# Softmax chain split between GpSimd and VectorE, units begun earlier, batch 1 loaded in 2 KB packets with v one block further ahead

## The chip, the cores and the metric

The kernel runs on one core of a Trainium2 chip. The metric is the time of one execution on the device, in microseconds (us). A core has several engines that run side by side (in the profile before, three of them are each busy for 85 to 95% of the same span): TensorE (PE in the profile; PEld is its weight load), VectorE (DVE), ScalarE (ACT), GpSimd (POOL) and SyncE (SP, which here only issues DMAs).

## The reference

Two layers follow one another, for 4 batches of 6208 rows with 256 channels:

```python
qn = q / (norm(q, axis=1) + 1e-6);  kn = k / (norm(k, axis=1) + 1e-6)   # norms over the 6208 rows
s  = kn.transpose(0, 2, 1) @ qn / tau                                    # 256 x 256 per batch
a  = exp(s - s.max(-1)); a /= a.sum(-1) + 1e-9
x  = v @ a                                                               # 6208 x 256 per batch
# channel mix, on x:
xk = mu_k * x + (1 - mu_k) * x_prev;  xr = mu_r * x + (1 - mu_r) * x_prev
out = sigmoid(xr @ w_r) * (relu(xk @ w_k) ** 2 @ w_v)                    # w_k: 256 x 1024
```

The matrix `a` of a batch is needed before the first row of that batch can be made, and it needs all rows of q and k of that batch.

## The kernel before

The rows of v are taken in 48 blocks of 512 rows, 12 to a batch (the 64 rows left over in each batch are put through in a last, shorter block). While the blocks of batch b go through the channel mix, the covariance of batch b+1 is built beside them in small *units*. One unit is 128 rows of q and k: two PE matmuls of 256 columns, and for every second unit a squaring on ACT and an addition on VectorE (for the norms). A block is written as eight steps (j = 0 to 7), and `slots` says at which steps a unit is put in. When the last unit of a batch is done, a *chain* of pieces is queued, one per step: it turns the sums into `a`. In short: `evac` copies the covariance out of PSUM, where this kernel's matmuls write it (`s_ps` in the profile); `fold` and `norms` sum the squares, `roots` copies these sums; `invert` makes the inverse norms and two diagonal matrices of them, `rq_d`; `turn` multiplies by these; `exp`, `shares` and `weigh` make the softmax.

```python
def invert():                                        # before, batches 1 to 3: all on GpSimd
    eng = nc.gpsimd if b else nc.vector
    if b:
        eng.tensor_tensor(rn, rn, half, op=OP.pow)   # rn is 128x4: root
    eng.tensor_scalar_add(rn, rn, 1e-6)
    if b:
        eng.tensor_tensor(rn, rn, minus, op=OP.pow)  # inverse
    else:
        eng.reciprocal(rn, rn)
    for h in range(2):                               # two 128x128 diagonals
        eng.tensor_scalar_mul(rq_d[:, h * P:(h + 1) * P], ident_f, rn[:, h:h + 1])
...
# the chain; `turn` is the PE product s_sb * rq_d that needs the diagonals, `weigh` writes a
return [evac, fold, None, None, norms, roots, invert, None, None, None, turn, exp, shares, weigh]
...
# q and k of a group of four units lie in SBUF as [unit, q|k, channel]: a DMA writes 512 B at a time.
# Groups for which apart() is true lie as [q|k, unit, channel]: 2 KB at a time,
# but here a squaring of two units is then two ACT instructions.
def apart(b, g):
    return b == 1 and g in (1, 2, 3)
...
if apart(b, g):
    for i in range(2):
        nc.scalar.activation(t[:rows, :, i * C:(i + 1) * C], rows_at(qk, b, g, i)[:rows, s:s + 2], AF.Square)
else:
    nc.scalar.activation(t[:rows], qk[:rows, s:s + min(n, 2)].rearrange("p s i c -> p s (i c)"), AF.Square)
...
# v: loaded by GpSimd, then transposed by a DMA that SP issues; x_half of block n runs in steps 0 and 2 of block n-2
if j == 0 and 4 <= i + 5 < NBLK - 1: v_load(i + 5)
if j == 5 and 4 <= i + 4 < NBLK - 1: v_transpose(i + 4)
...
# an addition of squares (VectorE) is issued at most at j = 1, 6, 7 (and at j = 2 when a chain waits for it)
```

## Time and profile before

| | before |
|---|---|
| time, median of 3 runs | 517.62 us (516.86 to 518.31) |
| span of the profile | 518.0 us |
| PE busy in the span | 494.2 us (95%) |
| GpSimd busy | 117.8 us |
| a block without units / with four / with six | 8.68 / 9.56 / 10.05 us |
| block 9, where batch 1's `turn` stands | 13.80 us |

The first part of the page (busy time of each engine, its share of the span, number of instructions) of the kernel before:

```profile
PE 494.2 (95%) x3478; PEld 337.3 (65%) x3540; DVE 438.4 (85%) x713; ACT 447.5 (86%) x906; POOL 117.8 (23%) x158
```

PE has little room: nearly everything that can be won is a hole in its row. The next view is the table of windows; here and below I cut the windows so that each is one block, from the first weight load of xr of that block to that of the next. The columns are named in the first line; (x73) counts instructions, PEclk is the granted clock of TensorE as a share of full speed. The three windows are block 5 (six units), block 7 (six units) and block 9 (five units and the `turn`) of the kernel before:

```profile
core 0: us, PE busy (x) PEld busy (x) DVE busy (x) ACT busy (x) POOL busy (x), PEclk, DMA share, GB/s
107.01:117.06 10.05, 10.00 (x73) 6.95 (x73) 10.05 (x16) 9.64 (x20) 2.40 (x4) 1.00 1.46 171
...
127.24:137.23 9.99, 9.88 (x71) 7.03 (x72) 9.99 (x16) 9.96 (x21) 1.49 (x2) 1.00 1.33 188
...
147.18:160.98 13.80, 11.14 (x78) 7.80 (x78) 8.72 (x14) 9.62 (x24) 10.19 (x12) 1.00 0.93 142
```

In blocks 5 and 7 of the kernel before PE is busy all but 0.05 to 0.1 us, and about that much is a matmul whose record the trace lost (725 records of one matmul line with 784 weight loads), not idleness. VectorE is busy for the whole block too: two engines are at their limit at once. In block 9, PE is idle for 2.66 us. The reason stands in PE's timeline there (start, length, then engine, line, operation, shapes, count, and in brackets the idle time before it and what ended it):

```profile
147.94 0.38 PE L182 MATMUL s_ps<-qk 128*128 128x256 bf16 x2
150.65 0.49 PE L275 MATMUL st_ps<-rq_d,s_sb 128*128 128x128 f32 x2 [2.33 <-POOL rq_d L263]
151.42 0.94 PE L275 MATMUL st_ps<-rq_d,s_sb 128*128 128x128 f32 x6 [0.28 <-POOL rq_d L263]
```

PE waits 2.33 and 0.28 us for the diagonals `rq_d`. GpSimd's timeline of the same stretch shows why they are late:

```profile
143.02 1.51 POOL L256 TENSOR_TENSOR rn<-rn,half 128x4 f32<-128x4 f32 x1 [10.97 <-ACT rn L251]
144.63 1.82 POOL L257 TENSOR_SCALAR rn<-rn 128x4 f32<-128x4 f32 x1
146.53 2.32 POOL L259 TENSOR_TENSOR rn<-rn,minus 128x4 f32<-128x4 f32 x1
148.96 2.41 POOL L263 TENSOR_SCALAR rq_d<-ident_f,rn 128x128 f32<-128x128 f32 x2
```

From the start of the first to the end of the last, these small steps take 8.3 us. In batch 0 VectorE does the same add, reciprocal and diagonals in 0.17, 0.18 and 2 x 0.28 us. For batches 2 and 3 GpSimd needed 5.6 and 4.9 us, and PE lost only about 0.3 and 0.15 us.

### The profile page before, as it was taken

Reading aid. Unit: us, or ns where it says so; the run is one execution under the profiler, and the core shown is the slowest. Engines: PE = TensorE matmul, PEld = TensorE weight load, DVE = VectorE, ACT = ScalarE, POOL = GpSimd, SP = SyncE. Lnnn points to the kernel's source line nnn. Section 1 sums busy time; section 2 is a strip of 40 time slices with the busy share of each in tenths; the row PEclk is TensorE's granted clock in tenths of the full one; section 3 lists DMA queues with packets and bytes.
Section 4 is the critical chain, followed back from the end, with each engine's and each line's share of the span. In section 5 each row is a group of like instructions: output and inputs, shape, how many; then the busy total and the mean of one; then the engine's idle time right before and its main releaser. Section 6 shows DMA issues by size and latency. Waiting matters only on the chain. (4 is left out here: it accounts for less than half of the span.)

```text
span 518.0 us, 9424 instructions
## 1 busy us (share of the span) xinstructions
PE 494.2 (95%) x3478; PEld 337.3 (65%) x3540; DVE 438.4 (85%) x713; ACT 447.5 (86%) x906; POOL 117.8 (23%) x158
## 2 busy tenths in 40 slices
PE   3979999999979999999999999999999999999996
PEld 2455666676656676667666666667666666666665
DVE  3555899999968999999988999999978888887884
ACT  5886999999969999999989999999878787878884
POOL 0034342322175221321155131210042101000000
PEclk9979999999999999999999999999999999999999
DMA  8989999999959999999559999965339686524123
GB/s 320 410 285 191 180 167 185 204 192 174 169 106 168 221 172 180 157 164 165 105 92 197 218 183 166 188 116 131 62 96 190 100 149 102 127 63 121 42 82 101
DMA packets 140373, 83.45 MB, mean 161 GB/s; under 512 B 50660, under 2 KB 135976, under 8 KB 140328
## 3 DMA queue, kind: packets, MB, share of 16 engines
q0 software_dynamic: 63504, 33.01, 51.5%
q1 hardware_dynamic: 76656, 49.72, 40.8%
q8 instruction: 27, 0.44, 0.4%
q14 instruction: 18, 0.15, 0.1%
q10 hardware_dynamic: 168, 0.13, 0.1%
HBM read 78.71 MB, written 25.43 MB: 201 GB/s over the span
## 5 line engine op out<-in xcount | busy, mean ns | idle before, releaser
L431 ACT ACTIVATE kr<-kT_ps 128x512 bf16<-128x512 f32 (+1 forms) x392 | 234.7, 607 | 36.9 <-PE kT_ps L426 28.6
L463 PE MATMUL vr_ps<-w_v_sb,kk 128*128 128x256 bf16 x1536 | 231.2, 273 | 0.5
L426 PE MATMUL kT_ps<-xk,w_k_sb 128*128 128x512 bf16 (+1 forms) x725 | 218.8, 377 | 0.7 <-DVE xk L411 0.5
L463 PEld LDWEIGHTS <-kk 128*128 128x128 bf16 x1536 | 149.1, 98 | 59.7 <-DVE kk L444 2.0
L473 DVE SCALAR_TENSOR_TENSOR res<-res,vr_ps 128x256 f32<-128x256 f32 x192 | 80.2, 418 | 48.1 <-ACT res L472 47.8
L444 DVE TENSOR_TENSOR kk<-kr 128x1536 bf16<-128x1536 bf16 (+2 forms) x148 | 117.4, 793 | 1.7 <-ACT kr L431 1.7
L426 PEld LDWEIGHTS <-w_k_sb 128*128 128x128 bf16 x784 | 75.8, 98 | 29.4 <-issue 1.2
L169 DVE TENSOR_TENSOR acc<-acc,sq 128x1024 f32<-128x1024 f32 x69 | 84.3, 1221 | 0.0
L182 PE MATMUL s_ps<-qk 128*128 128x256 bf16 x392 | 74.8, 293 | 5.4 <-DVE qk L142 5.4
L472 ACT ACTIVATE res<-vr_ps 128x256 f32<-128x256 f32 x192 | 76.9, 400 | 1.3 <-PE vr_ps L463 1.3
L459 PE MATMUL vr_ps<-w_r_sb,xr 128*128 128x256 bf16 x384 | 73.3, 272 | 3.3 <-DVE res L473 0.6
L411 DVE SCALAR_TENSOR_TENSOR xr<-delta,mu_t,xT 128x512 bf16<-128x512 bf16 x96 | 71.7, 749 | 0.0
L411 DVE SCALAR_TENSOR_TENSOR xk<-delta,mu_t,xT 128x512 bf16<-128x512 bf16 x96 | 71.6, 747 | 0.0
L165 ACT ACTIVATE sq<-qk 128x1024 f32<-128x1024 bf16 (+1 forms) x67 | 70.8, 1057 | 0.0
L459 PEld LDWEIGHTS <-xr 128*128 128x128 bf16 x384 | 37.6, 98 | 45.6 <-issue 2.0
L357 ACT CAST xT<-xT_ps 128x512 bf16<-128x512 f32 x94 | 55.6, 591 | 10.5 <-PE xT_ps L355 10.5
L136 POOL DMA_DIRECT2D qk<-in_q_dram x39 | 28.1, 721 | 157.0 <-ACT kr L431 127.1
L355 PE MATMUL xT_ps<-vT,a_sb 128*128 128x512 bf16 x188 | 55.9, 379 | 0.8 <-DVE vT L338 0.8
L182 PEld LDWEIGHTS <-qk 128*128 128x128 bf16 x392 | 39.9, 104 | 17.7 <-issue 6.3
L318 POOL DMA_DIRECT2D v_bf<-in_v_dram x48 | 37.5, 782 | 59.5 <-DMA vT<-v_bf 56.4
L401 DVE TENSOR_TENSOR delta<-xT 128x1024 bf16<-128x1024 bf16 x48 | 33.0, 688 | 1.9 <-ACT xT L357 1.8
L144 ACT ACTIVATE qk<-f 128x1024 bf16<-128x1024 f32 (+2 forms) x28 | 26.1, 948 | 8.7 <-DMA f<-in_q_dram 5.2
(85 smaller groups left out, 208.4 us busy)
## 6 DMA issues: line engine op xcount, KB each, us to landing
out_dram<-res SPq DMA_DIRECT2D x47, 512.0 KB, 5.0
v_bf<-in_v_dram POOLq DMA_DIRECT2D x48, 256.0 KB, 7.0
qk<-in_q_dram POOLq DMA_DIRECT2D x36, 256.0 KB, 7.5
qk<-in_k_dram POOLq DMA_DIRECT2D x36, 256.0 KB, 8.1
f<-in_q_dram SPq DMA_DIRECT2D x11, 512.0 KB, 8.6
f<-in_k_dram SPq DMA_DIRECT2D x11, 512.0 KB, 9.7
vT<-v_bf SPq DMA_TRANSPOSE x44, 6.5
f<-in_q_dram SPq DMA_DIRECT2D x2, 256.0 KB, 9.1
```

What stands on the lines that cost most here:

```text
L165: nc.scalar.activation(t[:rows], qk[:rows, s:s + min(n, 2)].rearrange("p s i c -> p s (i c)"), AF.Square)
L169: nc.vector.tensor_tensor(sums[b], sums[b], t, op=OP.add)
L182: nc.tensor.matmul(s_ps[:, ih, :], rows_at(qk, b, g, 0)[:rows, s, ih * P:(ih + 1) * P], rows_at(qk, b, g, 1)[:rows, s, :], start=t0 and ih ...
L355: nc.tensor.matmul(xT_ps, a_sb[:, b, ih, dh * P:(dh + 1) * P], vT[:, :, ih, :], start=ih == 0, stop=ih == 1)
L411: nc.vector.scalar_tensor_tensor(o[:, dh], st[i, "d"][:, dh], mu[:, dh:dh + 1], st[i, "x"][:, dh, :M], op0=OP.mult, op1=OP.add)
L426: nc.tensor.matmul(kT_ps[:, :m], w_k_sb[:, dh, fh * P:(fh + 1) * P], xk[:, dh, :m], start=dh == 0, stop=dh == 1)
L431: nc.scalar.activation(kr, kT_ps[:, :m], AF.Relu, scale=0.5 ** 0.5)
L444: nc.vector.tensor_tensor(st[i, "kk"][:, fh // 4 * 4 + lo:fh + 1, :m], kr, kr, op=OP.mult)
L459: nc.tensor.matmul(vr_ps[:, D:], xr[:, dh, s * P:(s + 1) * P], w_r_sb[:, dh, :], start=dh == 0, stop=dh == 1)
L463: nc.tensor.matmul(vr_ps[:, :D], kk[:, fh, s * P:(s + 1) * P], w_v_sb[:, fh, :], start=fh == 0, stop=fh == 7)
L472: nc.scalar.activation(res[:, s], vr_ps[:, D:], AF.Tanh, scale=0.5)
L473: nc.vector.scalar_tensor_tensor(res[:, s], res[:, s], 1.0, vr_ps[:, :D], op0=OP.add, op1=OP.mult)
```

## The change

Its intent is to take GpSimd's slow small steps out of the chain (only the power of the roots stays there, and `shares`, which the change does not touch), to begin the chain earlier so that nothing waits for it, to load batch 1 in fewer, larger packets, and to load and transpose v one block earlier. The diff, cut to its core:

```diff
-        return b == 1 and g in (1, 2, 3)
+        return b == 1 and g > 0
...
+        def pow2():
+            nc.gpsimd.tensor_tensor(rn, rn, half, op=OP.pow)
+
         def invert():
-            eng = nc.gpsimd if b else nc.vector
-            ... (as shown above)
+            nc.vector.tensor_scalar_add(rn, rn, 1e-6)
+            nc.vector.reciprocal(rn, rn)
             for h in range(2):
+                nc.vector.tensor_scalar_mul(rq_d[:, h * P:(h + 1) * P], ident_f, rn[:, h:h + 1])
...
-        return [evac, fold, None, None, norms, roots, invert, None, None, None, turn, exp, shares, weigh]
+        return [evac, fold, None, None, norms, roots, pow2, None, invert, None, None, turn, exp, shares, None, weigh]
...
-        v_bf = p2.tile(..., tag="v_bf", bufs=5)          # and vT: bufs=4
+        v_bf = p2.tile(..., tag="v_bf", bufs=6)          # and vT: bufs=5
...
-    FOLD = 13
+    FOLD = 15
...
-            if j == 0 and 4 <= i + 5 < NBLK - 1:
-                v_load(i + 5)
+            if j == 0 and 4 <= i + 6 < NBLK - 1:
+                v_load(i + 6)                            # and v_transpose(i + 5) for v_transpose(i + 4)
...
-            if (i, j) in ((-1, 6), (0, 4)):
+            if (i, j) in ((-1, 5), (0, 4)):              # PE transposes of v blocks 2 and 3
...
-            elif i < 8:
-                slots = (1, 2, 3, 4, 5, 7)
+            elif i < 7:
+                slots = (1, 2, 3, 4, 5, 7) if i < 3 else (1, 2, 3, 4, 5, 6, 7)
+            elif i == 7:
+                slots = (1, 2, 7)
+            elif (i - 7) % NB == 0:
+                slots = (5, 7)
             else:
-                slots = (3, 5, 7) if (i - 8) % NB == 0 else (1, 3, 4, 5, 7) if (i - 8) % NB < 3 else (1, 3, 5, 7)
+                slots = (1, 3, 4, 5, 7) if (i - 7) % NB in (1, 3, 6, 9) else (1, 3, 5, 7)
```

More of the change, by code (lines that the diff above doesn't have):

```diff
@@ L251, in roots @@
                 nc.scalar.copy(rn, bank[b][:, C:C + 4])
+        def pow2():
+            nc.gpsimd.tensor_tensor(rn, rn, half, op=OP.pow)
         def invert():
-            eng = nc.gpsimd if b else nc.vector
-            if b:
-                eng.tensor_tensor(rn, rn, half, op=OP.pow)
-            eng.tensor_scalar_add(rn, rn, 1e-6)
-            if b:
-                eng.tensor_tensor(rn, rn, minus, op=OP.pow)
-            else:
-                eng.reciprocal(rn, rn)
+            nc.vector.tensor_scalar_add(rn, rn, 1e-6)
+            nc.vector.reciprocal(rn, rn)
             for h in range(2):
-                eng.tensor_scalar_mul(rq_d[:, h * P:(h + 1) * P], ident_f, rn[:, h:h + 1])
+                nc.vector.tensor_scalar_mul(rq_d[:, h * P:(h + 1) * P], ident_f, rn[:, h:h + 1])
             if inv_tau != 1.0:
-                eng.tensor_scalar_mul(rk, rk, inv_tau)
+                nc.vector.tensor_scalar_mul(rk, rk, inv_tau)
         def evac():
@@ L316, in v_load @@
         b, t = blocks[i]
-        v_bf = p2.tile([P, S, C], BF16, name="v_bf", tag="v_bf", bufs=5)
+        v_bf = p2.tile([P, S, C], BF16, name="v_bf", tag="v_bf", bufs=6)
         nc.gpsimd.dma_start(v_bf, v[b, t * M:(t + 1) * M, :].rearrange("(s p) c -> p s c", p=P))
@@ L323, in v_transpose @@
         v_bf = st.pop((i, "v"))
-        vT = p2.tile([P, S, 2, P], BF16, name="vT", tag="vT", bufs=4)
+        vT = p2.tile([P, S, 2, P], BF16, name="vT", tag="vT", bufs=5)
         nc.sync.dma_start_transpose(vT.rearrange("c s h p -> c (s h) p"), v_bf.rearrange("p s c -> p (s c)"))
@@ L336, in go @@
         def go():
-            vT = p2.tile([P, S, 2, P], BF16, name="vT", tag="vT", bufs=4)
+            vT = p2.tile([P, S, 2, P], BF16, name="vT", tag="vT", bufs=5)
             evac(vT, vT_ps)
@@ L649 @@
                 mix(i + 1, "xr", int(j > 0))
-            if (i, j) in ((-1, 6), (0, 4)):
+            if (i, j) in ((-1, 5), (0, 4)):
                 v_transpose_pe(i + 3, nc.vector.tensor_copy)()
-            if j == 5 and 4 <= i + 4 < NBLK - 1:
-                v_transpose(i + 4)
+            if j == 5 and 4 <= i + 5 < NBLK - 1:
+                v_transpose(i + 5)
             if i == -1 and j in (5, 6):
```

## The prediction

> **What bounds the kernel now.** TensorE's streaming. The page has PE busy 95% of 518.0 us; the windows view 19.8 to 19.9 of every 20 us from 60 to 140 us and from 180 us on, clock 1.00. In the timeline matmuls start 0.11 us (256 columns) or 0.21 us (512) apart. By the output stores a block takes 8.68 us without covariance units (a unit = two 256-column matmuls), 9.55 with four, 10.05 with six. Only holes can be won:
> - Chain of batch 1 (timeline): PE waits from 148.0 to 150.65 us for rq_d from GpSimd, and 0.28 more: about 2.8 us. GpSimd: power 1.51, add 1.82, power 2.32, diagonals 2.41. Batches 2 and 3 lose only 0.3 and 0.15 us there.
> - At 55 us PE waits 0.83 us for VectorE's copy vT.
> - Batch 1's blocks: VectorE is never idle from 80 to 140 us. Its start-to-start times per block (4 res 0.33, 3 adds 1.136, 4 mixes 0.662, delta 0.60, squares 0.87 + 2 x 0.60) sum to 10.05 us, exactly the block; PE alone needs about 9.98 and waits some 0.05 for kk.
>
> [...] GpSimd's four-element add took 0.69 or 1.83 us.
>
> **What the change does.**
> - Inverse and diagonals on VectorE: 0.17 + 0.18 + 2 x 0.28 us (as in batch 0) in place of some 6.5 us on GpSimd; one power (1.2 to 1.5 us) stays. Norms to rq_d: about 6 us instead of 10.5; the turn comes seven steps (8.5 us) after the norms. So it waits for nothing: -2.8, -0.3, -0.15 us.
> - Units earlier: 7 per block in blocks 3 to 6, then 3 and 5; PE's work is the same in sum. But at most three adds are issued per block, so the fold waits to step 7 of block 7, and blocks 7 and 8 carry three adds each (before: three and one), plus fold (0.6) and inverse (0.7). VectorE then needs 10.65 and 10.75 us where PE needs 9.3 and 9.8; 0.6 us was regained in blocks 3 to 6. PE should lose 1 to 2 us there: most of what the stall gives back.
> - 2 KB packets: nine more groups are squared as two 512-column ACT instructions (0.52 us each, start to start) instead of one of 0.947: +0.09 x 18 = 1.7 us of ACT, which then needs about 10.1 us of a 10.2 us block; loss 0 to 0.5 us. PE waits for no q/k load before, so the packets give nothing themselves.
> - v one block further ahead: PE waits for no transposed load now: insurance, 0.
> - Transposes of v block 2 a step sooner: v landed at 49.7 us, needed at 51.4: -0.5 us.
>
> **Sum.** -2.8 - 0.5 (start) - 0.45 (batches 2, 3) - 0.6 (small vr_ps and kk waits) + 1.5 (VectorE, blocks 7, 8) + 0.2 (ACT): -2.7 us. Predicted **514.9 us**, 80% range **512.8 to 517.0**. Faster by over 2%: 0.01; within 2%: 0.97; slower: 0.02.
>
> **What would show it.** PE's waits for rq_d gone; GpSimd busy below 105 us; blocks 3 to 6 at 10.2 us; blocks 7 and 8 longer than 9.33 and 9.77 us with VectorE never idle; PE's wait at 55 us below 0.4 us.
>
> **What would make it wrong.** VectorE's lag reaching rq_d; ACT falling behind in blocks 3 to 6 (up to +2 us); VectorE's backlog absorbed by buffers (513 us); earlier v loads delaying q/k loads at the start.

The sum: -2.65 us, rounded to -2.7, from 517.6 to 514.9.

## More of the kernel before

One more line, which I passed over when I predicted and which turned out to matter, from the view of the tile vT (the transposed v): the time of its DMA transposes from issue to landing.

```profile
DMA to landing us min/median/max: 3.9/6.5/13.0
```

## The result, and the profile after

The time after was 514.26 us in the median (514.06 to 515.71, 4 runs), before 517.54 us (516.86 to 518.31, 4 runs). A ratio here is always the mean time of one kernel's runs over that of the other's runs of the same rounds, so it is not quite the ratio of the medians that I quote. The ratio is 0.9942, with a 95% interval of 0.9919 to 0.9965. The predicted 514.9 us lies 0.6 us off.

The span of the profile fell by more, 5.5 us, and a part of that is chance: the run of the kernel before that was profiled took 520.04 us, more than any of its four timed runs. I split every span at the first weight load of the up projection (w_k). What comes before is the phase in which DMA loads the first batch; it took 45.6 to 48.1 us in the profiles, with no order among kernels that share this code. What comes after, called the *main part* below, repeats: the changed kernel, profiled twice, gave 466.29 and 466.28 us, and one of the experiments, also twice, 465.77 and 465.75. Before, it was 470.17 us. So the change is worth 3.9 us in the main part of these traces; the kernel before has one trace only, and its wait for GpSimd varies by 2 us from trace to trace (see e11 below), so the 3.0 us by the ratio of the runs are the better figure.

The same part of the page for the changed kernel:

```profile
PE 494.6 (97%) x3540; PEld 336.7 (66%) x3540; DVE 439.7 (86%) x725; ACT 450.1 (88%) x924; POOL 99.9 (19%) x146
```

GpSimd is busy for 17.9 us less. PE at the turn of batch 1, and the chain's steps on the other two engines (from their timelines):

```profile
146.80 0.59 PE L352 MATMUL xT_ps<-vT,a_sb 128*128 128x512 bf16 x2
147.23 1.05 PE L272 MATMUL st_ps<-rq_d,s_sb 128*128 128x128 f32 x8
...
141.27 1.08 POOL L254 TENSOR_TENSOR rn<-rn,half 128x4 f32<-128x4 f32 x1 [15.55 <-ACT rn L251]
...
144.82 0.16 DVE L257 TENSOR_SCALAR rn<-rn 128x4 f32<-128x4 f32 x1
145.02 0.18 DVE L258 RECIPROCAL rn<-rn 128x4 f32<-128x4 f32 x1
145.23 0.48 DVE L260 TENSOR_SCALAR rq_d<-ident_f,rn 128x128 f32<-128x128 f32 x2
```

There is no wait in front of the turn: the diagonals are done at 145.7 us, and PE gets there at 147.2. But the windows of blocks 5, 7 and 8 show a new hole:

```profile
105.61:115.86 10.25, 10.25 (x76) 7.16 (x75) 10.25 (x16) 10.25 (x24) 2.81 (x4) 1.00 1.30 190
...
126.19:137.16 10.97, 9.80 (x67) 6.37 (x66) 10.97 (x17) 9.94 (x21) 0.00 (x0) 1.00 1.33 203
137.16:148.34 11.18, 11.18 (x88) 7.99 (x86) 11.11 (x21) 9.87 (x23) 3.36 (x4) 1.00 1.19 198
```

Block 5, now with seven units, has PE, VectorE and ACT all busy for its whole 10.25 us. Block 7 takes 10.97 us, of which PE is busy 9.80; without a wait it would need 9.43 (I take 8.67 us for a block without units and 0.218 for a unit, from the undisturbed blocks; this window holds 3.5 units). PE waits there for the results `res` of the block, which VectorE makes from ACT's output:

```profile
130.89 0.59 PE L423 MATMUL kT_ps<-xk,w_k_sb 128*128 128x512 bf16 x2
132.31 0.38 PE L456 MATMUL vr_ps<-w_r_sb,xr 128*128 128x256 bf16 x2 [0.82 <-DVE res L470]
```

And the landing of the transposes:

```profile
DMA to landing us min/median/max: 3.1/9.3/22.4
```

The slowest has gone from 13.0 to 22.4 us. The four issued from 57 to 90 us, in batch 1's blocks, took 18.5 to 22.4 us; before, those of that phase took 9.3 to 13.0 (as far as the trace has their landing).

Where the 3.9 us came from, by what each stretch lost against PE's own need (PE's own time for the norms and the turn, some 1.3 us per batch in both kernels, is in these sums):

| stretch | lost before | lost after | gain |
|---|---|---|---|
| main part up to block 0 (time, not loss) | 8.73 | 8.12 | 0.6 |
| blocks 0 to 2 | 1.1 | 1.5 | -0.4 |
| blocks 3 to 6 | 0.5 | 0.3 | 0.2 |
| block 7 (new hole) | 0.0 | 1.5 | -1.5 |
| blocks 8 to 11 (chain of batch 1) | 5.3 | 1.7 | 3.6 |
| blocks 19 to 23 (chain of batch 2) | 2.4 | 1.7 | 0.7 |
| blocks 30 to 33 (chain of batch 3) | 2.2 | 1.5 | 0.7 |

Two questions were open. Which part of the change brings the gain, and which only shifts it? And what causes the hole in block 7: VectorE's additions, as I had predicted (theory A), or ACT, which has no idle time left in blocks 3 to 6 because of the split squares (theory B)?

### The profile page after: what moved, and what is told of

The parts are those of the page before. It is cut to its first block, busy times and chain, and to the rows that moved or that the text cites. A ratio compares the mean times of both kernels' runs of the same rounds, so it can differ in the third digit from the quotient of the medians. Undisturbed runs are those within 1.5% of the kernel's fastest.

```text
span 512.5 us, 9496 instructions
## 1 busy us (share of the span) xinstructions
PE 494.6 (97%) x3540; PEld 336.7 (66%) x3540; DVE 439.7 (86%) x725; ACT 450.1 (88%) x924; POOL 99.9 (19%) x146
## 3 DMA queue, kind: packets, MB, share of 16 engines
q0 software_dynamic: 56592, 33.01, 50.0%
## 4 chain that ended last, share of the span: by engine, by line
PE 85%; DMA 6%; DVE 4%; ACT 4%; issue 1%; SPq 0%; DVEq 0%
PE vr_ps L460 31%; PE kT_ps L423 30%; PE vr_ps L456 8%; PE xT_ps L352 7%; PE s_ps L182 6%; DMA f<-in_k_dram 6%; ACT kr L428 1%; DVE acc L169 1%; DVE xk L408 1%; DVE kk L441 1%; PE st_ps L272 1%; ACT sq L163 1%; ACT xT L354 1%; DVE delta L398 1%; PE junk_ps L513 0%
## 5 line engine op out<-in xcount | busy, mean ns | idle before, releaser
L423 PE MATMUL kT_ps<-xk,w_k_sb 128*128 128x512 bf16 (+1 forms) x784 | 231.2, 377 | 0.4 <-DVE xk L408 0.2
L182 PE MATMUL s_ps<-qk 128*128 128x256 bf16 x392 | 73.5, 289 | 6.5 <-DVE qk L142 6.5
L354 ACT CAST xT<-xT_ps 128x512 bf16<-128x512 f32 x94 | 55.3, 589 | 12.1 <-PE xT_ps L352 12.1
L136 POOL DMA_DIRECT2D qk<-in_q_dram x39 | 26.3, 675 | 143.6 <-ACT kr L428 62.5
L165 ACT ACTIVATE sq<-qk 128x1024 f32<-128x1024 bf16 (+1 forms) x49 | 50.8, 1036 | 0.0
```

What stands on the lines that cost most here:

```text
L182: nc.tensor.matmul(s_ps[:, ih, :], rows_at(qk, b, g, 0)[:rows, s, ih * P:(ih + 1) * P], rows_at(qk, b, g, 1)[:rows, s, :], start=t0 and ih ...
L354: nc.scalar.copy(xT[:, dh, 1:], xT_ps)
L423: nc.tensor.matmul(kT_ps[:, :m], w_k_sb[:, dh, fh * P:(fh + 1) * P], xk[:, dh, :m], start=dh == 0, stop=dh == 1)
```

## The experiments

There were twelve kernels in three calls; those of one call shared a chip and the runs of the kernel before. On these chips the kernel before took 519.69, 517.88 and 518.77 us in the median.

| label | what it is | median us | ratio to before (95%) | main part us | block 7 us |
|---|---|---|---|---|---|
| before | | 517.5 to 519.7 | 1 | 470.17 | 9.99 |
| after | the change | 514.26 | 0.9942 (0.9919 to 0.9965) | 466.29 | 10.97 |
| e8_after_again | the change | 514.66 | 0.9945 (0.9922 to 0.9968) | 466.28 | 10.97 |
| e1_old_packets | change, packets undone | 513.55 | 0.9895 (0.9872 to 0.9919) | 465.93 | 10.62 |
| e2_inverse_only | before, VectorE inverse alone | 514.09 | 0.9897 (0.9875 to 0.9918) | 466.30 | 9.99 |
| e3_sooner_only | change, inverse on GpSimd | 519.94 | 1.0003 (0.9975 to 1.0031) | 471.16 | 10.71 |
| e4_two_adds_less | change, two additions left out | 513.69 (one run) | | 465.89 | 10.30 |
| e5_one_square | change, one ACT square per pair | 513.73 | 0.9935 (0.9907 to 0.9963) | 465.46 | 10.62 |
| e6_v_as_before | change, v no further ahead | 519.33 | 1.0035 (1.0011 to 1.006) | 471.97 | 10.72 |
| e7_parts_chosen | parts chosen | 513.30 | 0.992 (0.99 to 0.994) | 465.77 | 9.99 |
| e7_again | the same | 513.95 | 0.9915 (0.9888 to 0.9941) | 465.75 | 9.99 |
| e9_turn_step_1 | e7, turn one step sooner | 512.95 | 0.9902 (0.9874 to 0.993) | 465.21 | 9.99 |
| e10_both_less | e1 and e4 together | 513.28 (one run) | | 465.19 | 9.73 |
| e11_packets_only | before, packets alone | 522.24 (one run) | | 474.30 | 9.99 |

### The inverse alone (e2_inverse_only)

The kernel before, with the inverse and diagonals moved to VectorE, all else as it was; the turn keeps its place.

```diff
-        return [evac, fold, None, None, norms, roots, invert, None, None, None, turn, exp, shares, weigh]
+        return [evac, fold, None, None, norms, roots, pow2, None, invert, None, turn, exp, shares, weigh]
```
(with `pow2` and `invert` as in the change)

> The kernel before with one part of the change: power on GpSimd, inverse and diagonals on VectorE; same slots, same place of the turn. Theory A (the wait for GpSimd's rq_d is all that could be won from the chain, and the earlier start costs 1.5 us in block 7): PE's wait at the turn of batch 1 falls from 2.6 us to 0 to 0.5 us, blocks 1 to 7 stay at 10.05 us, the time is 2.5 to 3.5 us below before, so as good as the whole change or better by up to 1 us. Rival (the earlier start is needed): the turn still waits over 1 us for rq_d from VectorE, time 515.5 us or more.

PE's timeline at the turn of batch 1 in this kernel:

```profile
146.16 0.38 PE L182 MATMUL s_ps<-qk 128*128 128x256 bf16 x2
146.38 1.06 PE L272 MATMUL st_ps<-rq_d,s_sb 128*128 128x128 f32 x8
```

The wait is gone without any earlier start, block 7 has no hole (9.99 us), and the main part is 466.30 us, the same as the whole change. This confirms the theory: this one part brings what the whole change brings. (By the runs the ratio is even lower than the change's, but it was measured on another chip, and the intervals are wide; I do not build on that difference. The 5.6 us between the medians are also more than the 2.5 to 3.5 I had expected.) The two sums agree partly by chance: e2 has neither the 0.6 us that the change gains up to block 0 nor the hole that it pays in block 7.

### The earlier start alone (e3_sooner_only)

The changed kernel with the inverse back on GpSimd.

```diff
-  [evac, fold, None, None, norms, roots, pow2, None, invert, None, None, turn, exp, shares, None, weigh]
+  [evac, fold, None, None, norms, roots, invert, None, None, None, None, turn, exp, shares, None, weigh]
```
(with `invert` as before the change)

> The changed kernel with inverse and diagonals back on GpSimd (second power in place of the reciprocal). Theory A: GpSimd takes some 10 us from the norms to rq_d in batch 1, PE has 9.05 us of other work, so the turn of batch 1 waits 1 to 2 us, batches 2 and 3 wait under 0.3 us; block 7 keeps its 1.5 us hole; time 1 to 2 us above the changed kernel, about 515.8 us. Rival (sooner start is what removes the waits, the engine does not matter): no wait for rq_d, time 514.3 us or below, as VectorE is spared 0.7 us per chain.

The time was 519.94 us, no better than before, and 4 us worse than I had expected. Two waits of PE in its timeline explain most of it; a third, 0.61 us for rq_d in batch 3, where I had expected under 0.3, adds to it:

```profile
108.01 0.38 PE L355 MATMUL xT_ps<-vT,a_sb 128*128 128x512 bf16 x1 [1.64 <-DMA vT<-v_bf]
...
152.56 0.94 PE L275 MATMUL st_ps<-rq_d,s_sb 128*128 128x128 f32 x6 [2.15 <-POOL rq_d L263]
```

The second answers the question: the earlier start does not remove the wait for GpSimd. GpSimd's two diagonals alone took 4.85 us here, from 147.66 us on, where they had taken 2.41 before. The first wait was a surprise: PE waited for a transposed block of v, in a stretch where this kernel and the changed one are the same. The slowest transpose took 25.0 us. So the transposes became a suspect.

### Packets, and v further ahead (e1_old_packets, e6_v_as_before, e11_packets_only)

e1 is the changed kernel with the old packets. It was sent to tell theory A from B, but it answers this question too:

```diff
-        return b == 1 and g > 0
+        return b == 1 and g in (1, 2, 3)
```

> The changed kernel with batch 1's later groups in the old 512 B packets, so each of 18 squares is one 1024-column ACT instruction again. Theory A (VectorE alone has too much in block 7: three adds and the fold beside three units): block 7 still takes 10.9 to 11.0 us (PE needs 9.43), the time stays at 514.3 us, ratio 0.994. Rival B (ACT, never idle in blocks 3 to 6 because of the split squares, holds VectorE up and so causes part of the hole in block 7): ACT idle about 0.3 us per block in blocks 3 to 6, VectorE not idle at 120 us, block 7 at 10.5 us or less, the time 0.5 to 1.5 us less than the changed kernel.

e6 is the changed kernel with v loaded and transposed as before, and the 2 KB packets kept:

```diff
-            if j == 0 and 4 <= i + 6 < NBLK - 1:
-                v_load(i + 6)
+            if j == 0 and 4 <= i + 5 < NBLK - 1:
+                v_load(i + 5)                      # and v_transpose(i + 4), bufs 5 and 4
```

Its theory P is that the 2 KB packets double the time to landing of the transposes (from 57 to 115 us 11.5 us in the median before, 20.5 after).

> The changed kernel with v loaded and transposed no further ahead than before (2 KB packets kept). Prediction's view (v ahead is mere insurance): no wait of PE for a transposed load, time as the changed kernel. Theory P ([...] v ahead is what the packets cost): a transposed load is needed some 13.8 us after its issue, so PE waits for vT in blocks 3 to 7, 3 to 10 us in sum, time 517 to 524 us.

e11 is the kernel before with the 2 KB packets alone:

```diff
-        return b == 1 and g in (1, 2, 3)
+        return b == 1 and g > 0
```

> The kernel before with the 2 KB packets alone. Theory P (bigger packets beside the transposes double the transposes' landing, and v is not ahead): transposed loads take 15 to 21 us instead of 11 to 13, PE waits for vT in blocks 3 to 5, 3 to 7 us in sum, about 4 us slower than before, beside the unchanged 2.6 us wait for rq_d. Rival (packets harmless by themselves): PE waits for no vT, time within 1 us of before.

The view of the tile vT for e1, then for e6:

```profile
DMA to landing us min/median/max: 3.1/8.8/13.3
```

```profile
  DMA vT<-v_bf: 4.0, 2
...
DMA to landing us min/median/max: 3.9/5.7/20.9
```

The first line of e6's view says that PE sat idle twice before an instruction that reads vT, 4.0 us in all, until a transpose had landed. Its timeline has the longer of the two:

```profile
109.54 0.73 PE L352 MATMUL xT_ps<-vT,a_sb 128*128 128x512 bf16 x2 [3.21 <-DMA vT<-v_bf]
```

With the 2 KB packets the slowest transpose took 20.0 to 25.0 us in each of seven traces (after, e3, e4, e5, e6, e8, e11), with the old packets 13.0 to 13.7 in each of seven (before, e1, e2, e7 twice, e9, e10). With the 2 KB packets and v no further ahead, PE waits: e6 loses 5.7 us of its main part against the changed kernel (471.97 to 466.28; 4.7 us between the medians), e11 loses 4.1 against the kernel before (474.30 to 470.17), with 4.3 us of waits for vT in its trace:

```profile
  DMA vT<-v_bf: 4.3, 3
...
DMA to landing us min/median/max: 3.9/6.5/20.8
```

The waits are not the whole loss. In both traces the longest wait (3.21 and 3.59 us) is followed by 3.41 us in which the granted clock of TensorE is 0.50, as this window of e6 shows:

```profile
109.87:113.28 3.41, 3.41 (x14) 1.63 (x12) 2.07 (x3) 2.49 (x5) 0.00 (x0) 0.50 1.19 239
```

PE has 14 matmuls in it, and 27 in the next 3.41 us at clock 1.00; so up to 1.7 us more (half of 3.41, an estimate) were lost there. The slowest matmul that reads vT took 0.51 us in e6 and 0.63 in e11, and at most 0.39 in every other trace. Between the start of the main part and its last 1.5 us no other trace has such a stretch, with waits of PE of up to 2.33 us. That the wait brings it on is not shown.

So v one block further ahead is not insurance: it pays for what the larger packets cost. With the old packets there is nothing to pay for: e2 has v as before and no wait for a DMA transpose. And the larger packets themselves gave nothing that I could find: e1, without them, is 0.35 us shorter in its main part than the changed kernel.

How larger packets in one queue slow the transfers of another is not shown; what the traces show is this. The q and k loads run in GpSimd's queue and the transposes in SP's. In the profile's count the change left 6912 fewer packets in the first (56592 for 63504, by the page's part on queues), for the same bytes. From 57 to 115 us, by the traces' packet records, a 512 B packet of GpSimd's queue took 60 ns in the median before, and a 2 KB packet 172 ns after, while a 256 B packet in SP's queue took 31 ns in both. There the transposes took 20.5 us from issue to landing for 11.5 in the median, the output stores in the same queue 15.6 for 7.9, and the q loads themselves only 12.1 for 10.3. That the packets are the cause, the runs show; by what mechanism, they do not.

One expectation of e11 failed: its wait for rq_d was 0.48 and 0.09 us, not the unchanged 2.6, because GpSimd's steps took 6.3 us from start to end this time. GpSimd's times for the same instruction vary: the four-element add took 0.69 to 1.83 us, one diagonal 0.59 to 2.65 us; no run shows why. The 2.6 us wait of the kernel before is one draw of something that varies; in e3 it was 2.15. So e11's 4.1 us understate the packets' cost: with 2.0 us less of this wait, it lost 6.2 us in blocks 2 to 6, much as e6 did (5.9 in blocks 3 to 6).

### The hole in block 7 (e1_old_packets, e4_two_adds_less, e5_one_square, e10_both_less)

e4 takes away 2.27 us of VectorE's work and nothing else; its result is wrong:

```diff
+                if (i, j) in ((6, 6), (6, 7)):
+                    adds.pop(0)          # not added
+                else:
                     next_add()
```

> Wrong on purpose: the changed kernel without the two additions of squares at steps 6 and 7 of block 6 (2.27 us of VectorE, nothing else). Theory A: PE's waits for res (0.82 and 0.35 us, with their refilling 1.5 us) in block 7 vanish, block 7 takes 9.4 to 9.6 us. Rival B (ACT's backlog): block 7 stays above 10.5 us.

e5 keeps the 2 KB packets but squares a pair of units with one instruction again:

```diff
-            for i in range(2):
-                nc.scalar.activation(t[:rows, :, i * C:(i + 1) * C], rows_at(qk, b, g, i)[:rows, s:s + 2], AF.Square)
+            both = qk.rearrange("p s i c -> p (s i c)").rearrange("p (i s c) -> p i s c", i=2, s=S)
+            nc.scalar.activation(t[:rows].rearrange("p s (i c) -> p i s c", i=2), both[:rows, :, s:s + 2], AF.Square)
```

> The changed kernel with 2 KB packets, but each pair of units squared by one ACT instruction again (a pattern of two runs of 512 columns). If the ACT part of block 7's hole (1.54 us; 1.19 with the old packets) comes from the split squares and not from the packets' traffic: ACT idle 0.25 us per block in blocks 4 and 6, block 7 at 10.6 us, time 0.3 to 0.5 us below the changed kernel; the transposed loads still take about 20 us. If the packets' traffic itself matters, block 7 stays at 10.97 us.

e10 is e4 and e1 together, and also wrong:

```diff
-        return b == 1 and g > 0
+        return b == 1 and g in (1, 2, 3)
...
+                if (i, j) in ((6, 6), (6, 7)):
+                    adds.pop(0)          # not added
```

> Wrong on purpose: the changed kernel with both cuts, old packets (ACT's extra squares gone) and two additions less in block 6. If block 7's hole (1.54 us; 1.19 with the first cut, 0.87 with the second) is VectorE and ACT both being behind after the seven-unit blocks, both together leave 0.5 us or less. If a third cause holds the rest (the order of PE's own work with only three units between the res waits), 0.8 us stay.

Block 7 in the windows of e1, e4 and e10 (columns as above):

```profile
125.84:136.46 10.62, 9.66 (x68) 6.45 (x67) 10.62 (x16) 9.45 (x20) 0.00 (x0) 1.00 1.11 170
```

```profile
126.06:136.36 10.30, 9.66 (x68) 6.46 (x67) 9.65 (x15) 9.98 (x21) 0.00 (x0) 1.00 1.34 201
```

```profile
126.27:136.00 9.73, 9.44 (x66) 6.45 (x66) 9.08 (x14) 9.44 (x20) 0.00 (x0) 1.00 1.06 182
```

The changed kernel's hole was 1.54 us (10.97 less 9.43). Lighter squares on ACT bring it to 1.19, two additions less on VectorE to 0.87, both together to 0.31, whose cause stays open. Neither e1 nor e4 came out as either theory had said. So neither theory holds alone: after the four blocks with seven units both engines are behind, and with one of them relieved the other still holds PE up. In e1 VectorE is busy for all of the block; in e4 it has time to spare, 0.65 us, and in its timeline it waits twice for ACT's `res` around the start of block 7, 0.59 and 0.65 us. e5 shows that the ACT part is the squares' and not the packets' traffic: with the large packets and one square per pair, block 7 takes 10.62 us, just as in e1, though its slowest transpose still takes 20.0 us. One more sign of a backlog: in e3 and e6, where PE waited in block 4 and the other two could catch up, block 7 took only 10.71 and 10.72 us.

### A version of chosen parts (e7_parts_chosen, e7_again, e9_turn_step_1, with e8_after_again as base)

e7 keeps the inverse on VectorE, the earlier PE transpose of v block 2 and v further ahead; it puts batch 1's units and chain back where they were, drops the 2 KB packets, uses e5's single square, and spreads the later batches' fifth units:

```diff
+            elif i < 8:
+                slots = (1, 2, 3, 4, 5, 7)
+            elif (i - 8) % NB == 0:
+                slots = (3, 5, 7)
+            else:
+                slots = (1, 3, 4, 5, 7) if (i - 8) % NB in (4, 8) else (1, 3, 5, 7)
```

> Parts of the change chosen by the runs so far: inverse and diagonals on VectorE, transposes of v block 2 a step sooner, v one block further ahead; but the old packets, one ACT square per pair, batch 1's units and chain where they were (chain from block 8), and later batches' fifth units in the 5th and 9th block of a period. Theory: no hole in block 7 (9.99 us with six units), turn of batch 1 without a wait, blocks 9 to 11 without the 0.3 us waits; 1.5 to 2 us below the changed kernel, about 512.5 us where that takes 514.3. Rival (the earlier start is needed after all, because VectorE gives rq_d too late): a wait at the turn of over 0.5 us, time as the changed kernel.

> The changed kernel itself again, as the base of this chip. Both theories: block 7 at 10.97 us, transposed loads of v in batch 1 take 18 to 23 us from issue to landing (11 to 13 before), time 514.3 us on a chip like the first; its range shows whether a wait for a transposed load happens in some runs (as one of 1.6 us did in the sooner-only run).

e8, the changed kernel again, came out as expected in time (514.66 us) and block 7 (10.97); of its transposes from 57 to 90 us, two took 15.8 and 16.3 us and not 18 or more.

In e7 the hole in block 7 is gone (9.99 us), and the main part fell, but by 0.5 us against the changed kernel, not 1.5 to 2. Blocks 8 to 11 gave a part back: block 9 lost 0.91 us (the turn itself), block 10 0.54 and block 11 0.23, where the changed kernel, whose turn stands in block 8, lost 0.23, 0.02 and 0.02 (from block 8 to 11 in sum, 2.3 for 1.7). My reading was that e7's turn stands in step 2, in which PE also makes x for a later block, so that ACT first idles and then is late (in e7's block 9 ACT idles 0.67 and 0.38 us, and then VectorE waits 0.67 us for ACT's `res`). e9 tests it: norms, roots, power, inverse and turn all one step sooner.

```diff
-  [evac, fold, None, None, norms, roots, pow2, None, invert, None, turn, exp, shares, weigh]
+  [evac, fold, None, norms, roots, pow2, None, invert, None, turn, exp, shares, None, weigh]
```

> The version of chosen parts again, as base for the next one on the same chip: 0.7 to 1.3 us below the changed kernel's level, ratio to before about 0.992; blocks 9 and 10 lose 0.9 and 0.5 us to the turn and to a wait for res.

> As the chosen parts, with norms to turn one step sooner, so that the turn is at step 1 and not in step 2, where PE also makes x (both use the same PSUM tag, and ACT must take x and the exponentials one after the other; ACT idle about 1 us in block 9, then late with res in block 10). If that collision is what costs the 0.5 us in block 10 and 0.2 in block 11, they go, for each of three batches: 0.8 to 1.5 us less than the chosen parts. If it is ACT's load alone, nothing changes (within 0.2 us).

Blocks 9 to 11 now lose 0.02, 0.23 and 0.02 us, as they should if the collision was the cause. (e9 also puts one empty step between `shares` and `weigh`, as the change has it; the runs do not separate the two.) But the main part is only 0.54 us shorter than e7's, not 0.8 to 1.5, in part since the norms now come too soon after the fold:

```profile
140.25 0.25 PE L244 MATMUL bank<-ones,sq 128*128 128x1 bf16 x4 [0.59 <-DVE sq L237]
```

e9 has the lowest median with more than one run: 512.95 us where e7 took 513.95 and the kernel before 518.77. (By the ratio to the kernel before, e1 and e2, on another chip, are no worse: 0.9895 and 0.9897 for 0.9902.) By the runs its interval (0.9874 to 0.9930) is not clear of the changed kernel's (0.9922 to 0.9968); by the main part of the traces it is 1.07 us shorter (465.21 to 466.28). No version moves the time by 2%.

## Why the prediction was right

The time was predicted within 0.6 us and well inside the range. The sum was right partly by luck: two errors in it cancelled.

- **What bounds the kernel: right.** PE's need per block explained all undisturbed blocks to 0.1 us, so only holes could be won, and the change could not reach 2%.
- **The wait for the diagonals: right.** It was 2.6 us of idle PE in batch 1 and is gone; e2 shows that moving the inverse is enough, e3 that starting earlier is not. But the size came from one trace: e11, with the same inverse on GpSimd, waited 0.57 us.
- **The hole in blocks 7 and 8: size right, cause half right.** "PE should lose 1 to 2 us there": the hole in block 7 measured 1.54 us. I laid it to VectorE alone (ACT had a term of its own, 0.2 us); e10 with e1 and e4 shows that it is VectorE and ACT together. In block 8 nothing was lost: PE is busy for all of its 11.18 us, since norms and turn stand there too; I had left them out of PE's need, and they give VectorE the time for its inverse.
- **ACT's load: right.** I expected ACT to need about 10.1 us of a 10.2 us block; it is busy for all of blocks 3 and 5, and the nine further groups of split squares cost about 0.35 us (block 7 in e1 and e5). From start to next start, a square of 1024 columns took 0.95 us (before, at 88.38 us) and two of 512 columns 1.03 (after, at 86.67 us).
- **"v one block further ahead ... insurance, 0": wrong.** Without it the changed kernel loses 5.7 us of its main part (e6): 4.0 of waits for vT, and most of the rest in the stretch at half clock.
- **"the packets give nothing themselves": wrong in sign.** Alone they cost 4.1 us, or some 6 without the lucky draw of the wait for rq_d (e11). I had looked for waits on the q and k loads and found none, but not asked what larger packets do to the other queue. These are the two errors that cancelled: the change brings the cost and its cure together.
- **Start: mis-sized.** I gave it 0.5 us. PE's wait for vT fell from 0.83 to 0.22 us as expected, and up to block 0 the change brought 0.6, but blocks 0 to 2 lost 0.4 more. With one square per pair (e5) they lose 1.05 us and not 1.5, so the split squares on ACT, which the kernel before has in part, have a share in that.
- **Batches 2 and 3: mis-sized.** I predicted 0.45 us in all at the two turns, and 0.6 for small waits anywhere; the blocks around the two turns gained 1.4 us. Some of it is in the two blocks that follow a turn: in batch 2 they lost 0.36 and 0.37 us before (blocks 22 and 23), 0.22 and 0.19 after (blocks 21 and 22). e2 keeps these losses, so that part is not the inverse's.

## What to carry to other kernels

With PE full, an order in which two other engines are full as well had no give here: the four blocks of seven units (in block 5 all three engines are busy for 10.25 of 10.25 us) were paid for with a hole of 1.5 us in the block after them, and relieving one of the two engines left 1.19 or 0.87 us of it. Look for the smallest part of a change that brings its gain (here, four small operations moved to another engine: a main part of 466.30 us, for 466.29 with the whole change), since the other parts may only pay for each other (here the larger packets alone cost 4.1 us, and without v further ahead the changed kernel loses 5.7). Before making packets larger in one DMA queue, look at how long the other queues' transfers take and how late they may land (here the slowest transpose took 20.0 to 25.0 us with the larger packets and 13.0 to 13.7 with the old).
